# When the next chunk's gate/up weights are fetched in the W2 stage

## The chip, the cores and the metric

The kernel runs on one core of a Trainium2 chip. The metric is the device time of one execution in microseconds; the time before is the median of three runs. A core has TensorE (PE, with PEld for its weight loads), VectorE (DVE), ScalarE (ACT), GpSimd (POOL) and SyncE (SP). SP computes nothing here: it issues nearly all of the kernel's DMAs, one after the other, in the order of the program.

## The reference, cut to what matters

A token block of 2048 rows of 576 goes through a layer norm; attention with 32 heads of 18 and a window of 256 keys, and a gated MLP of width 4608, both read the normed rows, and their results are added to the input.

```python
def reference(A_x, A_wqkv, A_wo, B_x, B_w1, B_w3, B_w2):
    x = A_x
    xn = _layernorm(x, axis=-1)
    return x + _A_ref(xn, A_wqkv, A_wo) + _B_ref(xn, B_w1, B_w3, B_w2)
    ...
    # _B_ref, with F = 4608:
    gate = jnp.einsum("bsd,df->bsf", x, w1)
    up = jnp.einsum("bsd,df->bsf", x, w3)
    h = _silu(gate) * up
    out = jnp.einsum("bsf,fd->bsd", h, w2)
```

## The kernel before, in words

The 2048 rows are four chunks of 512. For each chunk `c` the program goes through three stages: the projection (q, k, v; in chunk 0 it stands ahead of the loop), the gate/up stage, and the W2 stage.

The **gate/up stage** has 36 units `u` of 128 hidden columns, each of nine pairs of matmuls (`unit_pairs`, L713) that read `xnT` and its half-swapped copy `xnS`. Scores, exponentials and the attention's products are put between them by a planner. The weights `w1` and `w3` come in nine sets of 512 columns a chunk, four units to a set. A set is six pieces of 192 KB; `load_part` issues the next piece of the next set, whatever chunk that belongs to (its DMA stands under L322 in the profile). There are three such buffers, so a set is fetched when the one that its buffer held has been used. During the gate/up stage the pieces are handed out two a unit; the first set of the next chunk is fetched so, late in the stage. The second set of the next chunk, for that chunk's units 4 to 7, is fetched in the W2 stage: its buffer was last read by units 28 to 31. That set is what the change moves. The third follows in the next projection.

The **W2 stage** multiplies the hidden rows `hT` with `w2`, adds the attention's output projection, and writes the chunk's rows. `p2_list` makes one list of items for it, and a loop takes them one by one (`p2_item`). The output's 576 columns are two halves of 288. In each half there are nine groups of 16 items, a group being one slice of `w2` of 288 KB, four 128-row pieces of it times four row tiles; each item is one matmul of 288 columns (L785). In the last group of a half each row tile's four matmuls are followed by four of the output projection (L792), and in half 0 by an `out` item: DVE adds the input rows (L803), and SP writes 72 KB (L805). So half 0 is items 0 to 163, its last group begins at item 128, and half 1 begins at item 164; in chunks 0 to 2 half 1 ends with four more matmuls (L699) and its four outputs. The `out` items take no time on PE.

The slices of `w2` have four buffers. The last item of a group calls `load_w2`, which issues the slice that is needed three groups later into the buffer that this group has just read (its DMA stands under L349); SP waits for that matmul first. The last four slices of the stage need no successor in it, so the last call that issues one comes after item 243.

The loop puts other things at fixed places of the list: the transposed send of the next chunk's last normed tile at item 40, input rows for the chunk after it at items 100 and 120, and at item 300 `xn_swap`, the two DMAs of 256 KB that make the next chunk's `xnS` (L426). A piece of the gate/up set is issued with `after=last_pe()`: SP waits until the latest matmul put into the program, that of the item at hand, is done. `xn_swap` has no such wait; it needs the next chunk's `xnT` and the end of the last read of `xnS`, both of which come earlier.

What sets the order around the change is therefore SP's queue in program order: the slices of `w2` (each waits for its buffer's last reader), the outputs (each waits for DVE), the pieces (each waits for its item), then `xn_swap`. PE waits for SP's work in one place only, at the first matmul of a group whose slice hasn't landed.

Of the kernel before, what the change touches and what calls it, by code (L numbers as in the profile page):

```python
# [164 lines left out]
def bass_parallel_sum__sliding_block__glu_gated_swiglu__prompt_kernel(  # L165
# [18 lines left out]
    NC = S // CH  # L184
# [13 lines left out]
    with ExitStack() as es:  # L198
# [95 lines left out]
        def load_x(t, eng="sp"):  # L294
            nonlocal xp_ctr
            s = xp_ctr % NXP
            xp_ctr += 1
            add(eng, lambda e: e.dma_start(xp[s][:], x2[t * 128:(t + 1) * 128, :]), w=[("xp", s)], dma=f"xp{s}")
            return s
# [11 lines left out]
        def load_part(after=(), behind=(), eng="sp"):  # L311

            nonlocal nfill
            if nfill >= 6 * NC * NFC:
                return
            k, i = divmod(nfill, 6)
            s, dst = w13_at(k)
            part, n = divmod(i, 2)
            c0 = (k % NFC) * 512
            src = (B_w3, B_w1)[n]  # L320
            nfill += 1
            add(eng, lambda e: e.dma_start(  # L322
                dst[64 * n:64 * n + 64, 3 * part:3 * part + 3, :],
                src[192 * part:192 * part + 192, c0:c0 + 512].rearrange("(kd p) f -> p kd f", p=64)),
                r=list(behind), after=after, dma=f"w13_{s}_{n}", **{"j" if i else "w": [("w13", s)]})
# [5 lines left out]
        def last_pe():  # L331
            return next(o for o in reversed(P.ops) if o.eng == "pe")
# [83 lines left out]
        def xn_send(t):  # L416
            i = t % 2
            c, tt = divmod(t, TB)
            add("sp", lambda e: e.dma_start_transpose(
                xnT[:, c % 2, :, tt * 128:(tt + 1) * 128], xn[i][:]),  # L420
                r=[("xn", i)], w=[("xnT", c % 2, tt)], dma=f"xnT{tt}")

        def xn_swap(c, eng):
            for n in range(2):
                p, q = 64 * n, 64 - 64 * n
                add(eng[n], lambda e, p=p, q=q: e.dma_start(  # L426
                    xnS[p:p + 64, :, :], xnT[q:q + 64, c % 2, 0:4, :]),
                    r=xk(c), dma=f"xnS{n}", **{"j" if n else "w": ["xnS"]})
# [223 lines left out]
        def pv_out(b, i):  # L652
            add("dve", lambda e, to=uqs[i]: e.transpose(to, PS[:, b, :]), r=[("ps", b)], w=uq_keys[i])  # L653

        def o_scale(i):
            u3 = uqs[i].rearrange("p (n d) -> p n d", d=32)
            o3 = oq[:, :].rearrange("p (n d) -> p n d", d=32)[:, :, 0:Dh]
            add("dve", lambda e: e.reciprocal(rden[:], u3[:, :, Dh]), r=uq_keys[i], w=["rden"])
            add("pool", lambda e: e.tensor_tensor(  # L659
                o3, u3[:, :, 0:Dh], rden[:].unsqueeze(2).to_broadcast([128, CH // 32, Dh]), ALU.mult),  # L660
                r=uq_keys[i] + ["rden", "oq0"], w=["oq"])

        def o_turn(g, half):
            i = g // 2 % NOD
            c0 = half * (CH // 2)
            add("dve", lambda e: e.transpose(od[i][:, g % 2, c0:c0 + CH // 2], oq[:, c0:c0 + CH // 2]),  # L666
                r=["oq", "oq0"], **{"j" if half or g % 2 else "w": [("od", i)]})
# [4 lines left out]
        def o_pack(j, eng):  # L672
            i = j % NOD
            first = True
            for q in range(4):
                m = 4 * j + q - 2
                if m >= 0:
                    t, r0 = 2 * (m // 7), Dh * (m % 7)
                    o_move(eng, oT[r0:r0 + Dh, t:t + 2, :], od[i][32 * q:32 * q + Dh, :, :], ("oT", j), first, f"oT{j}", [("od", i)])
                    first = False  # L680
# [278 lines left out]
        for c in range(NC):  # L959
# [195 lines left out]
            for n, item in enumerate(p2_list(c)):  # L1155
                p2_item(c, item, xs)
                if n == 3:
                    for u in sorted(side):
                        for what in side.pop(u):
                            what()  # L1160
                    pv_out(banks[0], 0)
                    pv_out(banks[1], 1)
                    o_scale(0)
                    o_turn(6, 0)
                    o_turn(6, 1)
                    o_scale(1)
                    o_turn(7, 0)
                    o_turn(7, 1)
                    o_pack(3, "act")
                elif 204 <= n <= 284 and n % 16 == 12 and c + 1 < NC:  # L1170
                    load_part((last_pe(),))
                elif n == 40 and c + 1 < NC:
                    xn_send((c + 1) * TB + 3)
                elif n == 300 and c + 1 < NC:
                    xn_swap(c + 1, ("sp", "sp"))
                elif n in (100, 120) and c + 2 < NC:
                    t = (c + 2) * TB + (n == 120)
                    xslot[t] = load_x(t)
# [31 lines left out]
```

## Time and profile before

| | |
|---|---|
| time, median of 3 runs (lowest to highest) | 557.83 us (557.51 to 559.01) |
| the profiled execution's own time | 557.61 us |
| its span | 555.9 us |
| granted TensorE clock | 1.00 |
| PE busy | 552.1 us (99%) |
| W2 matmuls (L785) | 1156, 146.7 us busy |
| slices of `w2` | 72 of 288 KB, median 3.3 us from issue to landing |
| gate/up pieces | 210 of 192 KB, median 3.9 us |
| second half of the W2 stage of chunk 0, 1, 2 begins at | 122.03, 259.11, 396.34 us |

The span is from the first to the last instruction of the profiled execution; 1.7 us of its time lie outside it. "Landing" is counted from the start of a DMA's issue on SP to the last of its completions. In rows of SP in order of time the columns are the start, the length of the issue, and the line; several issues of one line with nothing between them stand in one row (x3), whose length then holds the waits between them too.

### The profile page before, as it was taken

What the parts mean: (1) busy time and instruction counts of PE and PEld (TensorE: products, weight loads), DVE (VectorE), ACT (ScalarE), POOL (GpSimd) and SP (SyncE); (2) the same over time, 40 slices, a digit from 0 to 9 for tenths busy, and PEclk for the clock granted to TensorE, in tenths of its full rate; (3) what the DMA queues carried; (4) which work ended last, traced back from release to release, by engine and by line L of the source; (5) the groups of instructions that cost most, each with busy time, mean ns of one, the idle gap of its engine ahead of it and who ended that gap; (6) DMA issues with size and microseconds to landing.
All of it is one profiled execution on the core that took longest, in us unless ns stands there. A gap on an engine that the chain in (4) does not pass through costs nothing.

```text
span 555.9 us, 15754 instructions
## 1 busy us (share of the span) xinstructions
PE 552.1 (99%) x6772; PEld 346.6 (62%) x6772; DVE 311.4 (56%) x583; ACT 260.0 (47%) x359; POOL 162.7 (29%) x385
## 2 busy tenths in 40 slices
PE   8999999999999999999999999999999999999998
PEld 4666554677665545477766544847776554455776
DVE  6566978610365888851056687874105577678211
ACT  6457766100387774700048787550005777756000
POOL 5424534300034452530003454333001334333000
PEclk9999999999999999999999999999999999999999
DMA  9995989577377469756826748485582674553552
GB/s 244 201 206 139 211 188 243 106 196 186 90 143 164 114 138 167 217 136 174 203 57 140 169 126 198 123 205 136 151 187 54 138 174 122 150 151 82 142 150 65
DMA packets 127217, 85.96 MB, mean 155 GB/s; under 512 B 34452, under 2 KB 124908, under 8 KB 127148
## 3 DMA queue, kind: packets, MB, share of 16 engines
q1 hardware_dynamic: 125523, 83.49, 64.1%
q10 hardware_dynamic: 1624, 1.47, 1.0%
q8 instruction: 53, 0.87, 0.7%
q14 instruction: 17, 0.13, 0.1%
HBM read 71.29 MB, written 2.36 MB: 133 GB/s over the span
## 4 chain that ended last, share of the span: by engine, by line
PE 99%; ACT 0%; DVE 0%; issue 0%
PE ps L713 50%; PE ps L785 25%; PE ps L461 10%; PE ps L587 6%; PE ps L644 3%; PE ps L792 3%; PE ps L827 1%; PE ps L699 0%; PE ps L406 0%; ACT xnT L413 0%; DVE ofin L803 0%; DVE oq L821 0%
## 5 line engine op out<-in xcount | busy, mean ns | idle before, releaser
L713 PE MATMUL ps<-xnT,w 64*128 64x512 bf16 x1400 | 185.4, 376 | 0.0
L713 PE MATMUL ps<-xnS,w 64*128 64x512 bf16 x1120 | 154.0, 376 | 0.0
L785 PE MATMUL ps<-w,hT 128*128 128x288 bf16 x1156 | 146.7, 286 | 0.0
L728 DVE SCALAR_TENSOR_TENSOR gs<-th,ps 128x512 bf16<-128x512 bf16 x144 | 97.8, 679 | 76.6 <-ACT th L722 75.8
L785 PEld LDWEIGHTS ps<-w,hT 128*128 128x128 bf16 x1156 | 112.5, 98 | 28.9 <-issue 0.4
L713 PEld LDWEIGHTS ps<-xnT,w 64*128 64x128 bf16 x1400 | 73.0, 94 | 60.0 <-DVE ofin L653 0.2
L722 ACT ACTIVATE th<-ps 128x512 bf16<-128x512 f32 x144 | 85.6, 594 | 44.4 <-PE ps L713 42.0
L731 DVE SCALAR_TENSOR_TENSOR hT<-gs,ps 128x512 bf16<-128x512 bf16 x144 | 98.9, 687 | 4.9
L713 PEld LDWEIGHTS ps<-xnS,w 64*128 64x128 bf16 x1120 | 58.1, 94 | 46.7
L596 ACT ACTIVATE pt<-ps 128x1024 bf16<-128x1024 f32 (+1 forms) x70 | 70.8, 1011 | 31.2 <-PE ps L587 30.9
L474 ACT ACTIVATE stage<-ps 128x512 bf16<-128x512 f32 x16 | 9.5, 596 | 142.0 <-PE ps L461 142.0
L803 DVE TENSOR_TENSOR ofin<-ps,xp 128x288 bf16<-128x288 f32 x31 | 13.4, 455 | 108.3 <-PE ps L699 58.1
L623 POOL TENSOR_TENSOR hT<-hT,mk 128x128 int32<-128x128 int32 (+1 forms) x59 | 24.0, 429 | 170.5 <-ACT hT L596 170.3
L623 POOL TENSOR_TENSOR pt<-pt,mk 128x128 int32<-128x128 int32 (+1 forms) x124 | 49.9, 427 | 28.8 <-ACT pt L596 28.8
L587 PE MATMUL ps<-qv,kv 64*128 64x320 bf16 (+4 forms) x528 | 52.8, 260 | 0.0
L587 PEld LDWEIGHTS ps<-qv,kv 64*128 64x128 bf16 x528 | 27.4, 94 | 26.2 <-ACT hT L596 1.5
L596 ACT ACTIVATE w<-ps 128x1024 bf16<-128x1024 f32 (+1 forms) x32 | 32.3, 1010 | 12.3 <-PE ps L587 12.2
L461 PE MATMUL ps<-xnT,wp 64*128 64x512 bf16 (+1 forms) x360 | 38.0, 355 | 0.0
L596 ACT ACTIVATE hT<-ps 128x1024 bf16<-128x1024 f32 (+1 forms) x32 | 32.3, 1010 | 5.3 <-PE ps L587 4.8
L623 POOL TENSOR_TENSOR w<-w,mk 128x128 int32<-128x128 int32 (+1 forms) x56 | 22.9, 429 | 28.8 <-ACT w L596 28.8
L666 DVE STREAM_TRANSPOSE od<-oq 128x256 bf16<-128x256 bf16 x64 | 25.8, 427 | 6.9 <-POOL oq L659 6.9
L461 PEld LDWEIGHTS ps<-xnT,wp 64*128 64x128 bf16 x360 | 19.0, 94 | 14.4 <-ACT stage L474 0.2
(93 smaller groups left out, 384.9 us busy)
## 6 DMA issues: line engine op xcount, KB each, us to landing
w<-in_B_w_dram SPq DMA_DIRECT2D x210, 192.0 KB, 3.9
w<-in_B_w_dram SPq DMA_DIRECT2D x72, 288.0 KB, 3.3
xp<-in_A_x_dram SPq DMA_DIRECT2D x30, 144.0 KB, 4.5
out_dram<-ofin SPq DMA_DIRECT2D x31, 72.0 KB, 1.7
xnS<-xnT SPq DMA_DIRECT2D x8, 256.0 KB, 4.2
oT<-od SPq DMA_DIRECT2D x40, 36.0 KB
pt<-in_A_wqkv_dram SPq DMA_DIRECT2D x4, 288.0 KB, 6.0
hT<-in_B_w_dram SPq DMA_DIRECT2D x6, 192.0 KB, 5.2
```

The source lines that it names most:

```text
L461: op = add("pe", lambda e, out_=out_, st=st, mv=mv, n=n, r0=r0, first=first: e.matmul(out_, st, mv, start=first, stop=(part == 1 and n == ...
L587: add("pe", lambda e, r0=r0, out_=out_, kb=kb, q0=q0, nb=nb: e.matmul(out_, kb4[r0:r0 + 64, g, kb + NV - NB, :] if kb < 0 else kv[r0:r0 + ...
L596: add("act", lambda e: e.activation(pt_slot(sl)[:, 0:w, :], PS[:, SC[0]:SC[1] + 1, 0:w].rearrange("p r q -> p q r"), ACT.Exp, scale=scale) ...
L623: add("pool", lambda e, vb=vb, mm=mm: e.tensor_tensor(vb, vb, mm, ALU.mult), r=(key if n == 0 else []) + ["mk"], **{"w" if n == 0 else "j" ...
L644: add("pe", lambda e, p=p, q=q, pr=pr, sl=sl, g=g, pos=pos, q0=q0, nb=nb, col=col, first=first, n=n: e.matmul(PS[32 * q:32 * q + VW, banks ...
L666: add("dve", lambda e: e.transpose(od[i][:, g % 2, c0:c0 + CH // 2], oq[:, c0:c0 + CH // 2]), r=["oq", "oq0"], **{"j" if half or g % 2 els ...
L713: op = add("pe", lambda e, n=n, r0=r0, r=r, k=k, src=src: e.matmul(PS[:, b0 + r, :], wt[r0:r0 + 64, k, fl * 128:(fl + 1) * 128], src, star ...
L722: add("act", lambda e: e.activation(th[i][:], PS[:, bg, :], ACT.Tanh, scale=0.5), r=[("ps", bg)], w=[("th", i)])
L728: add("dve", lambda e: e.scalar_tensor_tensor(out=gs[i][:], in0=th[i][:], scalar=1.0, in1=PS[:, bg, :], op0=ALU.add, op1=ALU.mult), r=[("t ...
L731: add("dve", lambda e: e.scalar_tensor_tensor(out=hT[:, u, :], in0=gs[i][:], scalar=0.5, in1=PS[:, bu, :], op0=ALU.mult, op1=ALU.mult), r= ...
L785: add("pe", lambda e: e.matmul(bank, hT[:, f, tt * 128:(tt + 1) * 128], w2[sl][:, k, n0:n1], start=first, stop=(c + 1 == NC and half == 1 ...
L792: add("pe", lambda e: e.matmul(bank, oT[:, k, tt * 128:(tt + 1) * 128], wo[:, k, d0 + n0:d0 + n1], start=False, stop=(k == 3 and (half == ...
```

## The change

The condition that places the six pieces in the loop over the W2 items is changed. Before, the items whose number is 12 over a multiple of 16 are 204, 220, 236, 252, 268 and 284; after, they are 140, 156, 172, 188, 204 and 220. The first two then lie in the last group of half 0, among its outputs. Chunk 3 has no next chunk and is as before.

```diff
@@ -1167,7 +1167,7 @@
                     o_turn(7, 0)
                     o_turn(7, 1)
                     o_pack(3, "act")
-                elif 204 <= n <= 284 and n % 16 == 12 and c + 1 < NC:
+                elif 140 <= n <= 220 and n % 16 == 12 and c + 1 < NC:
                     load_part((last_pe(),))
                 elif n == 40 and c + 1 < NC:
                     xn_send((c + 1) * TB + 3)
```

## The prediction

> **What bounds the kernel now.** I read the page first, then the busy times by stretch.
>
> ```profile
> span 555.9 us, 15754 instructions
> PE 552.1 (99%) x6772; PEld 346.6 (62%) x6772; DVE 311.4 (56%) x583; ACT 260.0 (47%) x359; POOL 162.7 (29%) x385
> ...
> PE 99%; ACT 0%; DVE 0%; issue 0%
> ```
>
> ```profile
> 20.00:560.00 540.00, 533.49 (x6577) 337.02 (x6571) 298.75 (x552) 248.45 (x336) 148.94 (x353) 1.00 0.64 150
> ```
>
> The chain that ended last is 99% TensorE. The second row is the stretch from 20 us to the end: of the 535.9 us that the span has left there, PE is busy 533.49 at a granted clock of 1.00, so 2.4 us of it are idle, the tail after the last matmul included. Nothing in the middle of this kernel waits, so an edit of DMA times can hardly save anything; what it can do is make PE wait where it doesn't now.
>
> The only thing that PE needs from the queue in the W2 stage is the next 288 KB slice of `w2` (L349), four buffers deep. So I read the chain of waits in order of time for the pace, then the SP queue in order of time, for chunk 1, which has the tightest case.
>
> ```profile
> 259.11 16.17 PE ps L785 x132
> ...
> 396.34 16.17 PE ps L785 x132
> ```
>
> ```profile
> 255.22 0.37 SPq L349 DMA_DIRECT2D w<-in_B_w_dram  x1
> 256.69 2.29 SPq L805 DMA_DIRECT2D out_dram<-ofin  x3
> 259.03 0.43 SPq L349 DMA_DIRECT2D w<-in_B_w_dram  x1
> 259.63 0.38 SPq L805 DMA_DIRECT2D out_dram<-ofin  x1
> 261.10 2.35 SPq L349 DMA_DIRECT2D w<-in_B_w_dram  x2
> 264.16 0.69 SPq L322 DMA_DIRECT2D w<-in_B_w_dram  x1
> 265.02 0.47 SPq L349 DMA_DIRECT2D w<-in_B_w_dram  x1
> 266.12 0.66 SPq L322 DMA_DIRECT2D w<-in_B_w_dram  x1
> 266.98 0.44 SPq L349 DMA_DIRECT2D w<-in_B_w_dram  x1
> 268.08 0.60 SPq L322 DMA_DIRECT2D w<-in_B_w_dram  x1
> 268.94 0.39 SPq L349 DMA_DIRECT2D w<-in_B_w_dram  x1
> 270.04 4.51 SPq L322 DMA_DIRECT2D w<-in_B_w_dram  x3
> 274.67 1.18 SPq L426 DMA_DIRECT2D xnS<-xnT  x2
> ```
>
> The two chain rows are the second halves of the W2 stage in chunks 1 and 2, unbroken: 132 matmuls in 16.17 us, 0.1225 us each, so a group of 16 items takes 1.96 us. In the SP rows L322 is a piece of the gate/up set and L349 a slice of `w2`. The slice issued at 268.94 is for the last group of the half, which begins 128 items after 259.11, at 274.79: **a budget of 5.85 us** from issue to need, and the same for each slice that is released in step, since each is issued when the last reader of its buffer is done and needed three groups later.
>
> How much of the budget is used now stands in the landing times of L349, for the three slices of each chunk that have pieces beside them: chunk 0 (all three), chunk 1 (two, then the third) and chunk 2 (the same).
>
> ```profile
> L349 SPq DMA_DIRECT2D w<-in_B_w_dram x3: 389/439/469, 127.9 to 131.9; - x3
> ...
> DMA to landing us min/median/max: 3.6/3.7/4.0
> ```
>
> ```profile
> L349 SPq DMA_DIRECT2D w<-in_B_w_dram x2: 439/456/473, 265.0 to 267.0; - x2
> ...
> DMA to landing us min/median/max: 3.9/4.0/4.0
> ```
>
> ```profile
> L349 SPq DMA_DIRECT2D w<-in_B_w_dram x1: 389/389/389, 268.9 to 268.9; - x1
> ...
> DMA to landing us min/median/max: 5.3/5.3/5.3
> ```
>
> ```profile
> L349 SPq DMA_DIRECT2D w<-in_B_w_dram x2: 436/455/474, 402.2 to 404.2; - x2
> ...
> DMA to landing us min/median/max: 4.2/4.3/4.3
> ```
>
> ```profile
> L349 SPq DMA_DIRECT2D w<-in_B_w_dram x1: 388/388/388, 406.2 to 406.2; - x1
> ...
> DMA to landing us min/median/max: 5.2/5.2/5.2
> ```
>
> The least that is left over is 5.85 - 5.3 = 0.5 us, at the third slice of chunk 1. The stage runs without a stall, but not with much room.
>
> **The change part by part.** *What moves.* In chunks 0, 1 and 2 six pieces of 192 KB go 64 items earlier; number and size stay. In SP's order the first now stands behind the first output of half 0, the second just ahead of the slice that is released after item 158, the other four each 7 items ahead of a slice. Counted from the rows above in steps of 1.96 us, chunk 1 issues pieces at about 257.1, 259.0, 260.2, 262.2, 264.2 and 266.1 in place of 264.16 to 273.9.
>
> *SP's time.* A piece holds SP 0.60 to 0.69 us. Ahead of a slice that comes 0.86 us later (264.16 and 265.02) this is hidden, as now. At item 156 it isn't: SP issues the third output at 258.65, then the piece from 259.0 to 259.7, and the slice that now goes out at 259.03 goes out at 259.7. Its group begins 48 items after 259.11, at 264.99, so its budget falls from 6.0 to 5.3 us. With the 3.9 to 4.0 us that a slice beside a piece takes in this chunk it lands 1.3 us early. Cost 0.
>
> *The load on the DMA engines.* A slice (295 KB in thousands of bytes) and a piece (197 KB) in 1.96 us are 250 GB/s.
>
> ```profile
> 130.00:134.00 4.00, 4.00 (x35) 3.19 (x33) 0.00 (x0) 0.00 (x0) 0.00 (x0) 1.00 1.02 251
> ```
>
> That row is such a stretch in chunk 0: 251 GB/s at a DMA share of 1.02, so the engines are just full. The Trainium skill ("DMA: Bandwidth & Descriptors", Specifications) gives the fabric 435 GB/s and one core's HBM about 358; by those figures 250 GB/s would leave an estimated 30% free, no queue could build up, and the change would cost nothing at all. The trace disagrees with its 1.02, and the measurement decides.
>
> Before, this load lasts three groups (pieces at 204, 220, 236 beside slices after 211, 227, 243); then three pieces run alone. After, it lasts longer. Items 128 to 163 hold 32 matmuls, 3.92 us, and move one slice, two pieces and four outputs of 72 KB: 960 KB, 251 GB/s, two full rounds. Then come four more (172, 188, 204, 220). So **six full rounds in place of three**, and five slices beside pieces instead of three. The price depends on whether lateness piles up. In chunk 0 the landing goes from 3.6 to 4.0 over three slices, 0.2 a slice. In chunk 2 it goes from 4.2 to 5.2, 0.5 a slice. Lower end: 4.0 + 2 x 0.2 = 4.4 us, and no stall. Upper end: 5.2 + 2 x 0.5 = 6.2, 0.35 us over the budget, a stall of that size. I take 0.3 a slice, nearer the first, because the engines are full but not overfull: 3.9 + 4 x 0.3 = 5.1 us, inside the budget. Cost 0, between 0 and 0.35 us in each of three chunks. A stall is paid once a chunk: pieces and slices are released by PE's items, so a stopped PE stops the queue too.
>
> *The transposed copy `xnS`.* Its two DMAs (L426) wait for no matmul of this stage; now SP reaches them at 274.67 because the last piece is ahead of them. After, they follow the slice of 268.94 at once, at about 269.4, 5.3 us earlier. They are queued behind the last slice, so none is delayed by them. Their reader is the next chunk's gate/up stage, behind the whole projection: no gain, no cost.
>
> *What earlier pieces bring.* The set belongs to units 4 to 7 of the next chunk; it waits in its buffer either way. The last three groups of the stage lose their pieces, but their PE had no wait to lose. Gain 0.
>
> Sum: 557.61 (the profiled execution, 555.9 of it the span) + 3 x (0 to 0.35), taken as 3 x 0.1 because that interval has no side below nothing, 557.9. The median of the runs shown, 557.83, is 0.2 above the profiled one, so this is no change: **557.9 us**. A measurement of this kernel tells 0.3%, 1.7 us, from nothing.
>
> **The rivals.** *Slower: a slice comes late in half 1.* Place: the slices issued beside the third to sixth piece, needed at the starts of groups 13 to 16. Besides the drift there are single steps. In chunk 1 the third slice is 1.3 us later than the second; in that stretch the queue that fetches instructions moved one packet:
>
> ```profile
> q8 instruction: 1, 0.02, 0.9%
> ```
>
> ```profile
> q8 instruction: 53, 0.87, 0.7%
> ```
>
> The first row is 264 to 272 us, the second the page's for the whole kernel. 0.9% of 16 engines' 8 us is 1.15 us on one engine, and a slice has landed only when the last engine's share has. The whole span has 53 such fetches, one in 10.5 us; a load of six rounds lasts 11.8 us, so nearly every chunk gets one inside it. The drift of 0.5 and one step make 6.2 + 1.15 = 7.35 us, 1.5 over budget; with the middle drift 5.1 + 1.15 = 6.25, 0.4 over. Three chunks give 1.2 to 4.5 us, middle 2.9: **560.5**, at most 562.1. It decides when the landing passes 5.85 us, and shows over 0.3% when it passes 6.4 in all three. For it: 0.5 us of room, full engines, twice as many rounds. Against it: chunk 0 and the fact that before's last pieces come down again by themselves.
>
> *Faster: the freed end of the stage or the earlier `xnS` lets the next chunk begin sooner.* The most it could take is PE's wait at the end of this stage:
>
> ```profile
> PEld ps L699 <- issue: 0.9, 4, 0.2
> ```
>
> It is 0.2 us in each stage, ended by issue and not by a transfer: 3 x 0.2 gives **557.0**, which is within 0.3%.
>
> *The change does nothing:* SP, busy or held by an output's wait, issues the pieces where it did. SP idles between its rows, and the outputs' waits end by 259.63; I see at most 0.6 us of delay. It would be 557.6, on the side of my forecast.
>
> **How the numbers follow.** No stall that counts (with the null case): 0.60. Late slices worth over 1.7 us: 0.37, since the step of 1.15 is likely to meet each chunk and only its place in the rounds decides. Faster by over 0.3%: 0.03, as PE has no such idle time. The forecast's own range is 556.9 to 558.9 (0 to 0.35 in three chunks, and 0.3 us on each side for the median of a few runs: 557.51 to 557.83 is how far the lower two of those shown lie apart). The slower case reaches 562.1; I cut at 561.6, which leaves about 0.1 out there and 0.03 below 556.9.
>
> **What would show it.** Right: PE rows of 16.17 us for 132 matmuls stay in chunks 0 to 2; landings of L349 reach about 5 us and stay under 5.85; L426 is issued some 5 us earlier; the DMA share is about 1 for 12 us from the end of half 0. Wrong: PE or PEld of L785 waits for `w`, and the second half's row is longer than 16.17 us, by what the slowest landing exceeds 5.85. If the stretch grows with no landing late, my model of the queue is wrong altogether.

## The result, and the profile after

The changed kernel takes **561.09 us** (median of 6 runs, 560.67 to 562.08) against 557.78 us for the kernel before (6 runs, 557.48 to 559.01): 3.3 us slower, a ratio of 1.0058 with a 95% interval of 1.0045 to 1.0071. The forecast value, 557.9 us and no change, was wrong. The rival on the other side, a slice of `w2` that comes late in half 1, is what happened; it stood at 560.5 us and a chance of 0.37. The time lies in the stated range only because that was stretched towards this rival; the forecast's own part of it ended at 558.9.

The page after, its span, busy times and chain:

```profile
span 559.9 us, 15754 instructions
...
PE 553.8 (99%) x6772; PEld 340.9 (61%) x6772; DVE 311.0 (56%) x583; ACT 260.0 (46%) x359; POOL 163.1 (29%) x385
...
PE 95%; DMA 5%; issue 0%; ACT 0%; DVE 0%
```

DMA is now 5% of the chain that ended last, where it had no share. PE still reads 99% busy. About half of a wait of 0.3 us disappears in that figure, because a matmul's modelled length (286 ns, at a pace of 122.5) covers 0.16 us of it; the weight loads show the whole of it. The chain of waits of PEld after:

```profile
PEld ps L785 <- DMA w<-in_B_w_dram: 4.9, 11, 0.8
```

Eleven times the first weight load of a group waited for its slice. What that cost is read best from the chain in order of time (start, length, what), the second halves of chunks 0, 1 and 2:

```profile
121.80 2.46 PE ps L785 x21
124.26 5.87 DMA w<-in_B_w_dram
130.18 2.15 PE ps L785 x16
132.34 6.63 DMA w<-in_B_w_dram
139.02 0.66 PE ps L785 x4
...
261.39 9.81 PE ps L785 x80
271.23 6.36 DMA w<-in_B_w_dram
277.63 0.66 PE ps L785 x4
...
399.35 7.85 PE ps L785 x64
407.23 6.63 DMA w<-in_B_w_dram
413.90 2.62 PE ps L785 x20
```

Before, each of these was one row of 132 matmuls and 16.17 us. Now the same 132 matmuls end at 139.68, 278.29 and 416.52, after 17.88, 16.90 and 17.17 us: 1.71 + 0.73 + 1.00 = **3.44 us** more, against 3.3 us between the medians. (The profiled execution itself, 561.59 us, is 4.0 above the one before: besides the 3.44, chunk 1's gate/up stage is 0.8 us longer, with a wait at L587 that a second profile of the same kernel has not, and the start is 0.2 us shorter.) The loss is in the place that the rival named.

The rows below are SP in order of time in chunk 1, then the landing of three slices there, issued at 262.0, 263.8 and 265.3:

```profile
263.85 0.60 SPq L349 DMA_DIRECT2D w<-in_B_w_dram  x1
264.49 0.60 SPq L322 DMA_DIRECT2D w<-in_B_w_dram  x1
265.35 0.39 SPq L349 DMA_DIRECT2D w<-in_B_w_dram  x1
...
271.70 1.18 SPq L426 DMA_DIRECT2D xnS<-xnT  x2
```

```profile
DMA to landing us min/median/max: 3.6/3.6/3.6
```

```profile
DMA to landing us min/median/max: 4.7/4.7/4.7
```

```profile
DMA to landing us min/median/max: 6.0/6.0/6.0
```

3.6, 4.7, 6.0: in this chunk each slice takes more than a microsecond longer than the one before it, until one passes the budget of 5.85 us. The next ones stay near it (5.8, 5.7, 6.4). Chunk 2 goes the same way (3.5, 5.2, 6.3). Chunk 0 begins with a step: its first slice beside pieces, issued at 122.42, takes 5.4 us at once, and the next three take 5.9, 6.3 and 6.7.

```profile
L349 SPq DMA_DIRECT2D w<-in_B_w_dram x4: 387/603/607, 122.4 to 127.7; - x4
...
DMA to landing us min/median/max: 5.4/6.1/6.7
```

A slice has 16 completions in the trace, and its landing is the last of them. The table has the middle one, the last but one and the last, in us from the issue:

| slice | median | 15th | last |
|---|---|---|---|
| before, chunk 0, issued at 124.03 | 2.9 | 3.0 | 3.6 |
| the change, chunk 0, 122.42 | 3.3 | 3.5 | 5.4 |
| the change, chunk 0, 127.71 | 4.9 | 6.3 | 6.7 |
| the change, chunk 1, 265.35 | 4.7 | 5.6 | 6.0 |
| the change, chunk 2, 407.23 | 4.8 | 5.3 | 6.6 |

So two things add up. The whole transfer becomes slower from round to round, and one or two of its sixteen parts come later still. In chunks 1 and 2 of this profile no 15th completion passes 5.85 us; it is the last one that PE waits for.

The busy times by stretch show the same from both sides, 126 to 138 us of chunk 0, after and then before:

```profile
126.00:138.00 12.00, 11.27 (x88) 7.98 (x87) 0.00 (x0) 0.00 (x0) 0.00 (x0) 1.00 1.07 218
```

```profile
126.00:138.00 12.00, 12.00 (x100) 9.58 (x99) 0.00 (x0) 0.00 (x0) 0.00 (x0) 1.00 0.74 194
```

In 12 us there are 88 matmuls in place of 100, at a granted clock of 1.00 in both: 12 x 0.1225 = 1.47 us of chunk 0's loss. The DMA share is 1.07 while 218 GB/s are moved. That is no measure of the most that the engines can give, since a waiting PE also asks for fewer slices, and the copy of `xnS` lies in this stretch.

### The profile page after: what moved, and what is told of

It reads as the page before. It is cut to its first block, busy times and chain, and to the rows that moved or that the text cites. A ratio compares the mean times of both kernels' runs of the same rounds, so it can differ in the third digit from the quotient of the medians.

```text
span 559.9 us, 15754 instructions
## 1 busy us (share of the span) xinstructions
PE 553.8 (99%) x6772; PEld 340.9 (61%) x6772; DVE 311.0 (56%) x583; ACT 260.0 (46%) x359; POOL 163.1 (29%) x385
## 3 DMA queue, kind: packets, MB, share of 16 engines
q10 hardware_dynamic: 1624, 1.47, 0.9%
## 4 chain that ended last, share of the span: by engine, by line
PE 95%; DMA 5%; issue 0%; ACT 0%; DVE 0%
PE ps L713 50%; PE ps L785 21%; PE ps L461 9%; PE ps L587 6%; DMA w<-in_B_w_dram 5%; PE ps L644 3%; PE ps L792 3%; PE ps L827 1%; PE ps L699 0%; PE ps L406 0%; ACT xnT L413 0%; DVE ofin L803 0%; DVE oq L821 0%
## 5 line engine op out<-in xcount | busy, mean ns | idle before, releaser
L785 PE MATMUL ps<-w,hT 128*128 128x288 bf16 x1156 | 148.4, 286 | 1.8 <-DMA w<-in_B_w_dram 1.5
L713 PEld LDWEIGHTS ps<-xnT,w 64*128 64x128 bf16 x1400 | 71.1, 94 | 62.0 <-DVE ofin L653 0.2
L713 PEld LDWEIGHTS ps<-xnS,w 64*128 64x128 bf16 x1120 | 56.7, 94 | 48.1
L587 PE MATMUL ps<-qv,kv 64*128 64x320 bf16 (+4 forms) x528 | 52.7, 260 | 0.6 <-issue 0.6
L587 PEld LDWEIGHTS ps<-qv,kv 64*128 64x128 bf16 x528 | 26.8, 94 | 27.6 <-issue 1.6
```

The costliest lines, as they stand in the source:

```text
L587: add("pe", lambda e, r0=r0, out_=out_, kb=kb, q0=q0, nb=nb: e.matmul(out_, kb4[r0:r0 + 64, g, kb + NV - NB, :] if kb < 0 else kv[r0:r0 + ...
L713: op = add("pe", lambda e, n=n, r0=r0, r=r, k=k, src=src: e.matmul(PS[:, b0 + r, :], wt[r0:r0 + 64, k, fl * 128:(fl + 1) * 128], src, star ...
L785: add("pe", lambda e: e.matmul(bank, hT[:, f, tt * 128:(tt + 1) * 128], w2[sl][:, k, n0:n1], start=first, stop=(c + 1 == NC and half == 1 ...
```

## The experiments

My theory after the result: the DMA engines are asked for more than they deliver, lateness adds up from slice to slice, and it is paid whenever a slice passes its budget. The rivals were the copy of `xnS`, which the change moves 5 us earlier without naming it, SP's order and its time per DMA, and a slice's place behind a piece in one queue. Ratios are against the kernel before, run on the same chip beside each.

| kernel | median, us | ratio (95%) |
|---|---|---|
| pieces at 140 to 220 (the change) | 561.09 | 1.0058 (1.0045 to 1.0071) |
| the same, second time | 562.27 | 1.0069 (1.0055 to 1.0083) |
| the change, copy held to item 300 | 560.15 | 1.0041 (1.0029 to 1.0053) |
| pieces at 172 to 252 | 562.01 | 1.0073 (1.0050 to 1.0096) |
| pieces at 172 to 252, copy held | 559.92 | 1.0034 (1.0021 to 1.0046) |
| pieces at 188 to 268 | 558.20 | 1.0007 (0.9998 to 1.0016) |
| pieces as before, copy at 244 | 558.39 | 1.0012 (1.0003 to 1.0021) |
| two pieces early (140, 156) | 558.20 | 1.0006 (0.9998 to 1.0015) |
| the change, every 32 items | 557.85 | 1.0004 (0.9995 to 1.0012) |
| the change, every 24 items | 558.62 | 1.0014 (1.0005 to 1.0023) |
| the change, a third of the bytes | 558.23 | 0.9999 (0.9991 to 1.0008) |
| the change, pieces on ACT's queue | 560.68 | 1.0042 (1.0026 to 1.0058) |
| the change, five buffers for `w2` | 569.87 | 1.0209 (1.0192 to 1.0227) |

### Only half 1

```diff
-                elif 140 <= n <= 220 and n % 16 == 12 and c + 1 < NC:
+                elif 172 <= n <= 252 and n % 16 == 12 and c + 1 < NC:
```

> The six pieces stand at items 172 to 252, so the two that lay among half 0's outputs are gone from there and five full rounds stay. Theory of the full engines (slice, piece and outputs ask for 250 GB/s, lateness adds up round by round and is paid at each group whose slice passes 5.85 us): the queue starts empty at 172, so fewer stalls than the 3.4 us of the changed kernel, 0.3 to 1.5 us in all, 558.1 to 559.3 us. Rival of the earlier xnS copy (the last slice of the half shares the engines with 512 KB that used to come later): the copy again comes after a piece (252), behind the last slice by 9 items, so no stall and 557.8. Rival of SP's order (the piece at item 156 holds the slice behind it up): that piece is gone, 557.8.

Measured: 562.01 us, a loss as large as the change's own. My number was a miss, and SP's order falls as the cause: no piece stands at item 156 here. That the pieces among half 0's outputs are gone saved nothing. What I had left out is that the last of the six pieces and the copy now press on the last slices; the next two experiments part them.

### The copy held back

```diff
-        def xn_swap(c, eng):
+        def xn_swap(c, eng, after=()):
...
-                    r=xk(c), dma=f"xnS{n}", **{"j" if n else "w": ["xnS"]})
+                    r=xk(c), after=after, dma=f"xnS{n}", **{"j" if n else "w": ["xnS"]})
...
-                    xn_swap(c + 1, ("sp", "sp"))
+                    xn_swap(c + 1, ("sp", "sp"), (last_pe(),))
```

> The changed kernel with the xnS copy held until item 300 is done, so that it comes when it came before; the pieces stay at 140 to 220. Full engines: only the stalls at the last group can go (0.22 us in chunk 0, 0.33 in chunk 1, at most 0.28 in chunk 2), 560.3 to 561.1 us. Rival of the earlier copy: all stalls go, 557.8.

Measured: 560.15 us, 2.3 above the kernel before. So most of the loss is the pieces'. The medians leave about 1 us for the copy, with intervals that overlap; the rows of the W2 stage say where. Its second halves are 0.68, 0.91 and 0.74 us longer than 16.17 here, where the change's were 1.71, 0.73 and 1.00: the copy's microsecond is in chunk 0, chunk 2 gains 0.3 from holding it, and chunk 1 nothing. The landing of chunk 0's last slice, in the changed kernel and in this one:

```profile
L349 SPq DMA_DIRECT2D w<-in_B_w_dram x1: 368/368/368, 132.3 to 132.3; - x1
...
DMA to landing us min/median/max: 6.6/6.6/6.6
```

```profile
L349 SPq DMA_DIRECT2D w<-in_B_w_dram x1: 368/368/368, 132.1 to 132.1; - x1
...
DMA to landing us min/median/max: 4.5/4.5/4.5
```

The slice is issued ahead of the copy in both. With the copy issued half a microsecond behind it, it lands 2.1 us later. Not all of that is the copy's: the slice issued at 126.1 landed after 6.3 us in the changed kernel and 5.7 here, before any copy was issued. The chain of waits of PEld in this kernel still has nine of the eleven waits:

```profile
PEld ps L785 <- DMA w<-in_B_w_dram: 3.5, 9, 0.9
```

### Half 1 with the copy held

The two edits above together.

> Pieces at 172 to 252 as in the first of these runs, and the xnS copy held until item 300. If the rounds of slice and piece make the loss, most of the 4.1 us stays, 559.5 to 561.5 us; if the copy right behind the last slice makes it, 557.8 to 558.5 us. From the changed kernel, where holding the copy gave 0.9 us back, I expect 560.5.

Measured: 559.92 us. Of the 4.1 us that pieces at 172 to 252 cost by the medians, the copy makes 2.1 and the five rounds of slice and piece 2.0. In the two profiles the second halves are 1.83, 0.61 and 0.56 us too long with the early copy and 0.37, 0.68 and 0.59 with the late one, so again the copy's part is all in chunk 0.

### The copy alone

```diff
-                elif n == 300 and c + 1 < NC:
+                elif n == 244 and c + 1 < NC:
                     xn_swap(c + 1, ("sp", "sp"))
```

in the kernel before, its pieces left at 204 to 284.

> The kernel before with its pieces at 204 to 284 and only the xnS copy moved: issued at item 244, right behind the last slice. It tries what the prediction held to cost nothing. If a transfer behind a slice can't delay it: 557.8. If it does, the last slice (4.0, 5.3 and 5.2 us in the three chunks) gets about 1.5 us later, as in the changed kernel against the one with the copy held, and one stall a chunk of up to 1 us follows: 558.4 to 560 us.

Measured: 558.39 us, a ratio of 1.0012; the loss is at most 0.2%. The stage hardly stalls here: the second half of chunk 1, the only one that isn't 16.17 us, reads

```profile
259.63 16.20 PE ps L785 x132
```

The medians lie 0.5 us apart, but the W2 stage of this profile shows only 0.03 of it, so the place of the rest isn't shown. After five or six rounds the early copy cost 1 to 2 us by the medians: a transfer behind a slice hurts when the slices are already late.

### Fewer rounds, and rounds further apart

```diff
# every 32 items
+                elif n in (140, 172, 204, 236, 268, 284) and c + 1 < NC:
# two early
+                elif n in (140, 156, 236, 252, 268, 284) and c + 1 < NC:
# 188
+                elif 188 <= n <= 268 and n % 16 == 12 and c + 1 < NC:
# every 24 items
+                elif 140 <= n <= 260 and n % 24 == 20 and c + 1 < NC:
```

> The six pieces at items 140, 172, 204, 236, 268, 284, so that from 172 on only every second slice has one beside it, about 200 GB/s. Full engines: landings of 3.5 to 4.5 us, no stall, 557.6 to 558.0 us, although two pieces stand at items of the changed kernel that lie before its stalls. Rival of SP's order: 557.8 too, as item 156 has no piece.

> Two pieces alone go early, 140 and 156, among half 0's outputs; the other four stand at 236, 252, 268, 284. Full engines: two rounds at 250 GB/s, then slices alone for four groups, in which the queue empties: at most one stall of 0.2 us, 557.7 to 558.1 us. Rival of SP's order, or of pieces that collide with the outputs: the slice after item 158 still goes out 0.6 us late, and the loss that begins there stays, 558.8 or more.

> Pieces at 188 to 268, one group earlier than in the kernel before: four slices beside pieces in place of three, and the xnS copy after the piece at 268, a group earlier. Lateness that adds up round by round: the fourth slice lands about 0.4 us later than before's third (4.0, 5.3, 5.2), and one stall of 0 to 0.5 us a chunk follows: 558.0 to 559.0 us, between the kernel before (204) and the start at 172 with the copy held (559.9). Rival, a threshold with no build-up: either 557.8 or as much as from 172.

> Pieces from item 140 on as in the changed kernel, but 24 items apart (140 to 260), so that slices and pieces ask for 295 KB in 1.96 us and 197 KB in 2.94 us, 217 GB/s in place of 250. If the loss is lateness that adds up only while the engines are full, it is gone: landings up to 5 us, 557.7 to 558.4 us. If it is due to where the pieces start, a good part stays, 559 us or more.

Measured: 557.85, 558.20, 558.20 and 558.62 us. The first three can't be told from the kernel before, though two of them issue pieces as early as the change does. So it isn't the place of the first piece; it is how many full rounds follow one another. Four rounds (188) leave the stage without a stall, with landings up to 5.5 us in chunk 2; five or six in a row don't.

The kernel with 24 items between pieces, 217 GB/s asked, is slower by 0.05 to 0.23%, a little more than I allowed for. Its profile has three waits, two of them in chunk 2, behind slices that landed after 6.6 and 7.0 us. Full engines don't explain these two: the DMA share from 398 to 402 us is 0.88, and half of the completions of both slices are in by 3.6 us, the 15th by 4.5; only the last one is so late. In the stretch from 398 to 404 us one instruction fetch ran beside them:

```profile
L349 SPq DMA_DIRECT2D w<-in_B_w_dram x2: 390/393/396, 398.2 to 400.2; - x2
...
DMA to landing us min/median/max: 6.6/6.8/7.0
```

```profile
q8 instruction: 1, 0.02, 1.0%
```

### The same DMAs with a third of the bytes

```diff
-                    load_part((last_pe(),))
+                    load_part((last_pe(),), kd=1)
...
-                dst[64 * n:64 * n + 64, 3 * part:3 * part + 3, :],
-                src[192 * part:192 * part + 192, c0:c0 + 512].rearrange("(kd p) f -> p kd f", p=64)),
+                dst[64 * n:64 * n + 64, 3 * part:3 * part + kd, :],
+                src[192 * part:192 * part + 64 * kd, c0:c0 + 512].rearrange("(kd p) f -> p kd f", p=64)),
```

> The changed kernel, with the same six DMAs at the same items but each with a third of its bytes (one of three 64-row pieces, 64 KB; the other two thirds of that set are left out, so the next chunk's units 4 to 7 work on old weights). Full engines: 183 GB/s in place of 250, landings of 3.2 to 4 us, no stall, 557.6 to 558.1 us. Rival, that the number of DMAs or SP's time for them makes the loss: nothing of it goes, 560.5 to 561.5 us.

Measured: 558.23 us beside 558.14 for the kernel before; the loss is gone, with SP issuing the same number of DMAs in the same order. The first row has the busy times in chunk 0 from 122 to 132 us here, the second those of the changed kernel; this kernel's landings follow.

```profile
122.00:132.00 10.00, 10.00 (x84) 8.00 (x82) 0.92 (x2) 0.00 (x0) 0.00 (x0) 1.00 0.63 166
```

```profile
122.00:132.00 10.00, 9.63 (x78) 7.27 (x76) 0.29 (x1) 0.00 (x0) 0.00 (x0) 1.00 1.01 229
```

```profile
L349 SPq DMA_DIRECT2D w<-in_B_w_dram x5: 367/583/587, 123.7 to 131.1; - x5
...
DMA to landing us min/median/max: 3.4/4.3/4.6
```

It is the bytes, or the time that the engines need for them, and not the number or order of SP's DMAs.

### The pieces in another queue

```diff
-                    load_part((last_pe(),))
+                    load_part((last_pe(),), (), "act")
```

> The changed kernel with its six pieces issued by ScalarE, which has nothing to do in this stage, so that pieces and slices are in different queues of the same 16 engines. Theory A, a slice is late because it stands behind a piece in its own queue: with a queue of its own it lands in 3.5 to 4.5 us and the loss goes, 557.7 to 558.5 us. Theory B, the engines are full whatever the queue: slices as late as in the changed kernel, 560.5 to 561.5 us.

Measured: 560.68 us, theory B's number. The slices no longer stand behind pieces in their own queue, and they are late all the same. The landings of six slices of chunk 2 (one of them has none on record), and PEld's waits:

```profile
L349 SPq DMA_DIRECT2D w<-in_B_w_dram x6: 368/379/512, 398.2 to 408.3; - x6
...
DMA to landing us min/median/max: 3.5/6.1/7.6
```

```profile
PEld ps L785 <- DMA w<-in_B_w_dram: 4.2, 6, 1.3
```

The pattern does change: six waits instead of eleven, and longer ones.

### A longer budget

```diff
-        NXP, NOF, NPT, NW13, NW2, NOD = 7, 4, 10, 3, 4, 2
+        NXP, NOF, NPT, NW13, NW2, NOD = 7, 4, 9, 3, 5, 2
...
-                if u in (range(27, 31) if c == 0 else range(JOINT[c][0] + 1, JOINT[c][0] + 8, 2)):
-                    load_w2(c * 2 * NFC + 4)
+                if u in (range(27, 32) if c == 0 else [JOINT[c][0] + k for k in (1, 3, 5, 7, 8)]):
+                    load_w2(c * 2 * NFC + 5)
```

> The changed kernel's schedule of pieces with five buffers for w2 in place of four, so that a slice is issued four groups ahead and has 7.8 us in place of 5.85 (one attention buffer less pays for the space). Full engines with a budget that is too small: the landings stay as long as in the changed kernel (5 to 7 us) or get a little longer, as PE no longer stops, but fit: 557.6 to 558.3 us. Rival, lateness that is held down only by PE's own stalls: without them it grows past 7.8 us and some of the loss comes back, 558.8 or more.

The whole time is no evidence: 569.87 us, since the planner has a buffer less and PE waits in other stages. Its values also differ from the reference's; by my reading of the program, one attention tile in chunks 1 to 3 is overwritten by the fifth slice before it is read, which no run shows. The second half of the W2 stage has the same matmuls and transfers. That half answers the question. Its rows in the chain, chunks 0 to 2, and chunk 0's landings of the slices beside pieces:

```profile
122.02 16.17 PE ps L785 x132
...
265.12 16.17 PE ps L785 x132
...
404.34 16.17 PE ps L785 x132
```

```profile
L349 SPq DMA_DIRECT2D w<-in_B_w_dram x5: 388/599/606, 122.6 to 129.9; - x5
...
DMA to landing us min/median/max: 5.3/5.6/7.2
```

Slices land as late as in the changed kernel, up to 7.2 us, and all three halves take 16.17 us. With one group's time more room, 1.96 us, no lateness is paid: the budget is the other half of the cause. The same pieces and slices, with no wait of PE among them, moved 245 GB/s from 122 to 132 us, where the changed kernel moved 229:

```profile
122.00:132.00 10.00, 10.00 (x84) 8.00 (x82) 0.46 (x1) 0.00 (x0) 0.00 (x0) 1.00 0.98 245
```

The rival, lateness that runs away without PE's stalls, isn't seen over these rounds: in chunk 1 the five slices take 3.5, 4.3, 5.2, 4.9 and 5.2 us.

### The change once more

> The changed kernel once more, beside the others on the same chip: 560.7 to 561.5 us, so that the runs with the copy held and with the pieces on another queue have a neighbour.

Measured: 562.27 us, somewhat above my range, beside 558.14 for the kernel before. The loss is 4.1 us here and was 3.3 in the first set; the intervals overlap. In the profile of this second time the three halves are 1.35, 0.71 and 0.83 us too long, 2.89 in all.

## Why the prediction was right or wrong

**What bounds the kernel, and the gains of zero:** right. PE had nothing to win; no kernel here is faster than the one before.

**The budget of 5.85 us:** right. The waits begin where landings pass it, 16.17 us rows stay where they don't, and a longer budget takes the waits away. The shorter budget of 5.3 us for the slice after item 158 was seen too, but its landing was put at 3.9 to 4.0. That held in chunks 1 and 2 (3.6 and 3.5); in chunk 0 it took 5.4 us, and the weight load that waited for it could begin only at 127.86.

**The drift of 0.3 us a slice, "because the engines are full but not overfull":** this is the step that failed. The forecast's 3.9 + 4 x 0.3 = 5.1 us for the fifth slice beside pieces came out at 6.8, 5.7 and 6.6 in the three chunks. In chunk 1 the first three slices rose by 1.1 to 1.3 us each and in chunk 2 by 1.7 and 1.1; in chunk 0 the start was 1.5 us too low and the rise 0.4 to 0.5. I had read 251 GB/s at a share of 1.02 as a load that the engines could hold, from a stretch of 4 us that ends by itself.

The load was also more than I had put it at. Outputs and pieces meet at the start of half 1: in chunk 1 SP issued three pieces, three slices and an output from 261.31 until the next piece at 266.45, 1.55 MB in 5.1 us, which is an estimated 300 GB/s. The kernel with pieces from 172 and the copy held has no such crowd. There the five slices rise from 5.5 to 6.0, 4.5 to 6.3 and 5.1 to 6.2, which is 0.1 to 0.5 a slice as forecast, but from a start that is 0.6 to 1.6 us higher than 3.9. Why it starts higher isn't shown.

**"A stall is paid once a chunk":** wrong. There were six, two and three waits in the three chunks. A stop of PE delays the next releases, but only by its own length, and the following rounds ask for as much as before.

**The copy of `xnS`, "none is delayed":** wrong. It was issued behind the last slice, at 271.70 in chunk 1 as forecast, and with it the slice ahead landed later: by the medians 1 to 2 us of the loss where slices were already late, in the profiles nearly all of it in chunk 0. Order of issue isn't order of landing.

**The rival's sum:** its 2.9 us against 3.3 is partly luck. In chunks 1 and 2 the drift came out larger than its 0.5 a slice. A single step on one of sixteen parts was there too, and larger than its 1.15 us: the first slice of chunk 0 had 15 completions by 3.5 us and the last at 5.4. The fetch that the rival made responsible did run then (from 122 to 132 us, below), but no run moved it. And the rival counted one stall a chunk. The mechanism, place and sign were those of the rival; the weights of the two cases were the wrong way round.

```profile
q8 instruction: 1, 0.02, 0.6%
```

**The Trainium skill's ceiling** ("DMA: Bandwidth & Descriptors", Specifications) of 358 GB/s from HBM would have given no loss. The runs show late slices at 218 to 245 GB/s, well under it; what the most is that this mix can get, no run shows. The same page of the Trainium skill (section "How a descriptor splits into AXI transactions") says that a run of 576 bytes that doesn't start on a 256-byte boundary costs more beats than one that does. The rows of a `w2` slice are 576 bytes, but no run here varied their length or place, so this is no more than a candidate.

**Open:** the waits differ from chunk to chunk in one kernel (1.71, 0.73 and 1.00 us). An instruction fetch of 16 KB falls into some of these stretches and not into others. Where it does, the last completion often stands alone: the fetch in the table's chunk 0 began at 124.6, and in the kernel with pieces from 188 the slice issued at 124.46, with a fetch from 125.5, has its 15th completion after 2.9 us and its last after 4.5. No run moved a fetch, so its share isn't shown, and the trace doesn't say which engine the last completion belongs to. How a copy delays a slice issued ahead of it, and why mainly in chunk 0, wasn't taken apart either.

## What to carry to other kernels

A prefetch that nobody waits for still takes the engines' time from one that somebody does; before moving it, add up the bytes asked for in each stretch, and take the rate to compare with from a stretch at least as long. Where the stream that matters has a fixed budget from issue to need, compare its landing times with that budget slice by slice: rising landings are the warning, and here two or three more rounds turned 0.5 us of room into a loss. Ask of a late landing whether the whole transfer is late or only its last part. Ask of each moved wait what else was kept in its place by it, as the copy was by the last piece.

## What the runs showed of the hardware

With a transfer issued half a microsecond behind it, a slice landed after 6.6 us in place of 4.5, while slices ahead of it were 0.6 us later already. The last of a transfer's 16 completions can be 1.9 us behind the 15th (3.5 and 5.4), and 2.7 in the kernel with 24 items between pieces (4.3 and 7.0). Issuing the pieces from ScalarE's queue didn't protect the slices left in SP's: 560.68 us against 561.09. In the kernel with five buffers the granted clock was 0.84 at the start of chunk 1's W2 stage, and its first half took 17.92 us in place of 16.28:

```profile
244.00:254.00 10.00, 10.00 (x71) 7.46 (x70) 2.94 (x8) 0.00 (x0) 1.35 (x2) 0.84 0.49 105
```
